# A transformer block on one core: row sums in column tiles of 32, three unused products at the passage to attention, and one subtraction moved to GpSimd

## The chip, the cores and the metric

The kernel runs on one core of one Trainium2 chip. The metric is the device time of one execution in microseconds (us). Engines are named as in the profile: PE is TensorE's matrix multiplication, PEld its weight load, DVE is VectorE, ACT is ScalarE, POOL is GpSimd, SP is SyncE, which issues nearly all DMAs.

## What is computed

A block of 2048 tokens by 576 features, in float32. Six vectors of modulation come from one row `c`; attention has 32 heads of 18 with one shared key and value; the mixer part is a two-layer MLP with a hidden size of 4608.

```python
mod = (silu(c) @ w_mod).reshape(1, 6, 1, 576)
sa, ca, ga, sb, cb, gb = (mod[:, i] for i in range(6))
h = layernorm(x) * (1 + ca) + sa
q, k, v = h @ wq, h @ wk, h @ wv                  # 32 heads of q, one of k and v
p = softmax(q @ k.T * 18 ** -0.5)
x = x + ga * ((p @ v) @ wo)
h = layernorm(x) * (1 + cb) + sb
x = x + gb * (gelu(layernorm(h) @ w1 + b1) @ w2 + b2)
```

## The kernel before, in words

The program is one long recording with the order of every engine written out by hand. It has three stages, each with its own division of the eight PSUM banks.

**Stage 1** (up to about 129 us) normalizes x, multiplies by the projection weights in four blocks of 512 tokens (`q_chunk`), and begins the row maxima that the softmax needs. A `unit()` is one such piece for the second quad of heads: four products (L319) into two double banks `psA`, and a `tensor_reduce` on DVE for each (L337). The last unit stands at the very end of the stage. `busy(n)` (L391) multiplies the identity by itself n times into a bank `psB` that nobody reads; the kernel uses it three times near the start.

**Stage 2** (129 us to about 1387 us) is attention, in 32 quads of four heads. A list of tokens (`QUAD`, later `QUADW`) sets the order: S is a product of scores (L901, into one of four banks `psB`, read by an exponential on ACT, L903), M a product for the maxima of the next quad (L319, into one of three banks `psM`, read by a reduction on DVE, L923), X a corrected maximum (L911, L914, L921), V a number of 128-column pieces of the product of probabilities and values. V has 32 stationary columns, so four of them stand side by side in column tiles of PE (L891). F1 and F2 finish the maxima of the next quad; F2 is one small transposing product (L357), so its record marks a fixed place in every quad. After every second block of keys a step of a list of side work (`fill`) is taken, just behind the V product. In the first quads the side work is `late_weights`: four of the modulation rows are made here, not in stage 1. POOL scales a 576 x 576 matrix by silu(c) and adds its five slices (L498, L501); what is left is a sum over 128 partitions, whose result every partition needs. `bcast` (L516 to L523) makes it: a product with a stationary 128 x 128 matrix of ones, 288 columns at a time into two banks (L521), and a `tensor_scalar` on DVE for each half (L522). Rows 5, 2 and 3 are made in the quad n = 1, row 4 in n = 2. Row 2 (`gab`) then scales the output weights (L550).

**Stage 3** (from 1387 us) is the MLP, for two halves of the tokens, with Strassen-like sums of blocks: `op_pieces` forms the operands from the normalized rows. `form("=T4")` is a subtraction of two 128 x 1024 blocks (L1016), `-B21` and the like are the low parts of operands (L1025). For the first half of the tokens `e2` is DVE for all sums; for the second half, formed in step v = 17, `e2` is POOL, and of the three subtractions only `=T1` runs on `e2`.

SP takes its DMAs in the order in which they are written; a DMA that waits keeps all later ones waiting. On SP stand in stage 2 the loads of queries (L315), the rows of maxima (L364), the modulation matrices (L527, L92) and the output weights (L540).

Of the kernel before, what the change touches and what calls it, by code (L numbers as in the profile page):

```python
# [32 lines left out]
def block_kernel(ctx: ExitStack, tc, x, wqkv, wo, w1, b1, w2, b2, c, wmod, ident_in, out):  # L33
    nc = tc.nc
    ve, ac, po, pe, sy = nc.vector, nc.scalar, nc.gpsimd, nc.tensor, nc.sync

    per = ctx.enter_context(tc.tile_pool(name="per", bufs=1))
    dr = ctx.enter_context(tc.tile_pool(name="dr", bufs=1, space=bass.MemoryType.DRAM))
# [14 lines left out]
    def psB(): return PS["t"].tile([128, 512], F32, name="psB", bufs=PS["b"])  # L53
# [3 lines left out]
    def big(): return per.tile([128, 10, 512], F32R, name="big", bufs=3)  # L57
# [17 lines left out]
    BC = per.tile([128, 3, D], F32, name="BC")  # L75
# [36 lines left out]
    unity = pa.tile([128, 128], F32, name="unity")  # L112
# [157 lines left out]
    def q_chunk(tb, m, zt, mid, n):  # L270

        w = 126 if m < KD - 1 else 128
        wd = 126 if m < KD - 1 else 72
        pq = psB()
        proj(pq[:w], wqh, wql, 126 * m, 126 * m + w, zt, mid, n)
        qs = p1.tile([128, 2, TB], F32R, name="qs", bufs=2)
        qf = p1.tile([128, TB], F32, name="qf", bufs=2)
        ac.activation(qf[:w], pq[:w], AF.Copy)
        ac.activation(qs[:w, 0], pq[:w], AF.Copy)
        po.tensor_tensor(qs[:w, 1], qf[:w], qs[:w, 0].bitcast(F32), op=ALU.subtract)  # L280
        if m == KD - 1:
# [47 lines left out]
    def smax_half(n, u, half):  # L329
        p, qt = UNITS[u]  # L330
        ts = psA(), psA()
        for i in range(2):
            for g in range(2):
                smax_mm(n, ts[g][:, i, :], g, p, qt, 2 * half + i)
        for g in range(2):
            k, ax = (slice(2 * half, 2 * half + 2), AX.X) if g == 0 or half == 0 else (slice(2, 3), AX.XY)
            ve.tensor_reduce(mx_tile(n)[:, 8 * g + 4 * p + qt, k], ts[g], axis=ax, op=ALU.max)  # L337
# [52 lines left out]
    def busy(n):  # L390

        p = psB()
        for _ in range(n):
            pe.matmul(p[:, :128], ident, ident, start=True, stop=True)
# [42 lines left out]
    def unit():  # L437
        nonlocal u1
        smax_half(1, u1 % 2, u1 // 2)
        u1 += 1  # L440
# [5 lines left out]
    for tb in range(NB):  # L446
        nz = big() if tb + 1 < NB else None
        for i, m in enumerate((4, 0, 1, 2, 3)):
            np_ = NPART[tb][i]
            if i == 2:  # L450
                parts.extend((u, tb) for u in range(8))
            mid = {(NB - 1, 1): unit, (NB - 1, 4): lambda: last.popleft()()}.get((tb, i), part)
            qf, qs = q_chunk(tb, m, zt, mid, np_ + 1 if np_ else 0)
            if i == 0:
                qv = qf, qs
            if i == 1:
                k_block(tb, qv[1])
                v_block(tb, qv[0])
                if tb == 0:
                    load_q(0)  # L460
            if i == 2:
                if tb == 0:
                    load_q(1)
            if tb == NB - 1:
                if i == 0:
                    unit()
                elif i == 3:
                    smax_fin1(0)
                if i == 4:
                    unit()  # L470
            if nz is not None:
                for k in {1: (0, 1, 2), 2: (3, 4)}.get(i, ()) if tb else {3: (0, 1, 2), 4: (3, 4)}.get(i, ()):
                    h_chunk(tb + 1, nz, k)
            if tb < 2:
                for _ in range(NSTAT[tb][i]):
                    ln1_stats(*stats.popleft())
                for _ in range(NAPPLY[tb][i]):
                    b, t = applies.popleft()
                    ln1_apply(b, t, ve if b == 1 else ac)
        zt = nz  # L480
# [5 lines left out]
    px = pxp.__enter__()  # L486
# [2 lines left out]


    WO, YR, ATT, B2 = {}, {}, {}, {}

    def late_weights():

        gab = pb.tile([128, D], F32, name="gab", tag="r2", bufs=3)

        def scaled(w, k0, k1):
            po.tensor_tensor(w[:, k0:k1], w[:, k0:k1], st[:, k0:k1, None].to_broadcast([128, k1 - k0, D]), op=ALU.mult)  # L498

        def added(w, k0, k1, n=1):  # L500
            po.tensor_tensor(w[:, k0:k0 + n], w[:, k0:k0 + n], w[:, k1:k1 + n], op=ALU.add)  # L501

        def total(w):

            scaled(w, 0, 2)
            yield
            scaled(w, 2, 4)
            yield
            scaled(w, 4, 5)
            added(w, 0, 2, 2)  # L510
            yield
            added(w, 0, 1)
            added(w, 0, 4)
            yield

        def bcast(w, dst, add, scl):  # L516

            for h2 in range(2):
                cs = slice(288 * h2, 288 * (h2 + 1))
                p = psB()  # L520
                pe.matmul(p[:, :288], unity, w[:, 0, cs], start=True, stop=True)  # L521
                ve.tensor_scalar(dst[:, cs], p[:, :288], scl, add, op0=ALU.mult, op1=ALU.add)  # L522
            yield  # L523

        m3, m2, m5 = (bigw(D) for _ in range(3))
        for j, t in ((5, m5), (2, m2), (3, m3)):
            sy.dma_start(t, wmod[j])  # L527
        yield
        sums = (x for t in (m5, m2, m3) for x in total(t))
        rows = (x for a in ((m5, BC[:, 2, :], 0.0, 0.5), (m2, gab, 0.0, 1.0), (m3, BC[:, 0, :], 0.0, 1.0))  # L530
                for x in bcast(*a))
        for i in range(12):
            for _ in range(2):
                next(sums, None)
            if i > 5 and i % 2:
                next(rows)
            yield
        m4 = load_mod(4)
        wor = bigw(D)
        sy.dma_start(wor, wo)  # L540
        ATT[0] = big()
        yield
        yield from total(m4)
        yield
        yield
        yield from bcast(m4, BC[:, 1, :], 1.0, 1.0)
        wos = pw.tile([128, 2, KD, D], F32R, name="wos", tag="wA", padded_shape=[128, 2, KD, WQC])
        WOH, WOL = WO["h"], WO["l"] = wos[:, 0], wos[:, 1]
        for k in range(KD):
            po.tensor_mul(wor[:, k, :], wor[:, k, :], gab)  # L550
            po.tensor_copy(WOH[:, k, :], wor[:, k, :])
            po.tensor_tensor(WOL[:, k, :], wor[:, k, :], WOH[:, k, :].bitcast(F32), op=ALU.subtract)
            yield
# [396 lines left out]
    for n in range(NQT):  # L950
# [54 lines left out]
    def op_pieces(R, e2):  # L1005


        at = {"B11": (0, 0, ve), "B21": (2, 2, e2), "B22": (4, 7, e2), "T2": (6, 5, ve), "T1": (8, 5, ve),
              "T3": (10, 0, ve), "T4": (12, 2, e2), "t0": (0, 4, ve), "t1": (1, 9, ve)}
        less = {"T3": (5, 0, 0), "T4": (2, 5, 2), "T1": (7, 5, 5)}  # L1010

        def form(what):
            for w in what.split():
                if w[0] == "=":
                    x, y, o = (R[:, i:i + 2] for i in less[w[1:]])
                    (e2 if w == "=T1" else ve).tensor_tensor(o, x, y, op=ALU.subtract)  # L1016
                    continue
                a, r, e = at[w[1:]]
                n = 2 if w[1] in "BT" else 1
                o, lo = (OP, 14) if n == 2 else (TL[0], 2)  # L1020
                hi, src = o[:, a:a + n], R[:, r:r + n]
                if w[0] == "+":
                    ac.activation(hi, src, AF.Copy)
                else:
                    e.tensor_tensor(o[:, lo + a:lo + a + n], src, hi.bitcast(F32), op=ALU.subtract)  # L1025
        return form
# [31 lines left out]
    px = ctx.enter_context(tc.tile_pool(name="mx", bufs=1, side="right", reuse_waits="tile"))  # L1058
# [256 lines left out]
    for v in range(NV):  # L1315
# [44 lines left out]
        bc = psB()  # L1360
# [111 lines left out]
```

## Time and profile before

| what | value |
|---|---|
| median of 3 runs | 2242.26 us (2241.82 to 2245.19) |
| profiled execution | 2243.08 us |
| its span, first to last instruction | 2241.3 us |
| outside the span | 1.8 us |
| busy PE, DVE, ACT, POOL | 2212.7, 1940.8, 1645.1, 1524.7 us |
| mean granted clock of TensorE | 0.998 |

A row of the timeline has the start, the time covered, engine, line, operation, tiles, shape and count; in brackets the idle time of the engine ahead of it and what ended that. A row of a window has the stretch, its length, the busy time of PE, PEld, DVE, ACT and POOL with their instruction counts, then the granted clock, the share of DMA time and GB/s. PE works on a float32 product in two passes, so one product of such operands has two records.

### The profile page before, as it was taken

The page shows a single profiled execution, that of the slowest core. Times are in us where ns is not written, and L with a number is a line of the kernel's source. Part 1 is how long each engine was busy: PE and PEld are TensorE (multiplying, and loading weights), DVE is VectorE, ACT ScalarE, POOL GpSimd, SP SyncE. Part 2 cuts the span into 40 slices and gives each one's busy share as a digit, 9 for nine tenths or more (in the row PEclk, how much of TensorE's full clock was granted, in tenths as well). Part 3 has the DMA queues.
Part 4 walks back from the last instruction along what each step waited for, and adds up shares of the span by engine and source line. Part 5 has one row for each costly group of instructions (what it writes and reads, how often), then busy time and mean ns, then how long its engine had stood idle before and what let it go on. Part 6 is the DMA issues. An engine that isn't in the chain of part 4 may idle for free.

```text
span 2241.3 us, 45781 instructions
## 1 busy us (share of the span) xinstructions
PE 2212.7 (99%) x16458; PEld 1442.2 (64%) x16458; DVE 1940.8 (87%) x3420; ACT 1645.1 (73%) x3145; POOL 1524.7 (68%) x1760
## 2 busy tenths in 40 slices
PE   7999999999999999999999999999999999999999
PEld 5644544444444544444444445888888888989898
DVE  7589999999999999999999982887888878888787
ACT  5569999999999999999999997444545544344443
POOL 6654356776877787777776300888888857877776
PEclk9999999999999999999999999999999999999999
DMA  6232034443433333343333101666666646676664
GB/s 229 85 129 75 15 114 138 133 142 110 138 121 126 121 122 115 124 139 115 117 127 127 49 13 48 194 177 179 180 178 176 190 122 181 182 213 191 177 183 125
DMA packets 182404, 303.79 MB, mean 136 GB/s; under 512 B 19243, under 2 KB 74923, under 8 KB 182177
## 3 DMA queue, kind: packets, MB, share of 16 engines
q1 hardware_dynamic: 182033, 300.72, 42.9%
q8 instruction: 130, 2.13, 0.4%
q14 instruction: 97, 0.79, 0.1%
q10 hardware_dynamic: 144, 0.15, 0.0%
HBM read 198.71 MB, written 93.19 MB: 130 GB/s over the span
## 4 chain that ended last, share of the span: by engine, by line
PE 86%; DVE 3%; ACT 3%; POOL 2%; issue 1%; DMA 0%; SPq 0%; POOLq 0%; ACTq 0%
PE psC L891 21%; PE psB L1111 18%; PE psA L1214 16%; PE psB L901 13%; PE psM L319 10%; PE psB L700 2%; ACT P L903 2%; PE psB L911 2%; DVE mx L923 1%; PE psA L1248 1%; PE psA L700 1%; DVE xc L921 0%; PE psB L155 0%; PE psB L357 0%; PE psB L248 0%
## 5 line engine op out<-in xcount | busy, mean ns | idle before, releaser
L903 ACT ACTIVATE P<-psB 128x512 f32<-128x512 f32 x2008 | 1043.8, 619 | 35.0 <-PE psM L319 12.3
L923 DVE TENSOR_REDUCE mx<-psM 128x1 f32<-128x512 f32 x1476 | 938.1, 683 | 37.5 <-PE psM L319 14.9
L319 PE MATMUL psM<-KS,qst 64*128 64x512 f32 x1722 | 601.2, 442 | 0.4 <-DVE mx L923 0.4
L901 PE MATMUL psB<-qst,KS 64*128 64x512 f32 x2008 | 585.1, 429 | 1.7 <-DVE mx L337 1.5
L891 PE MATMUL psC<-P,V 128*32 128x256 f32 (+3 forms) x6424 | 576.3, 448 | 0.5 <-ACT O L715 0.5
L901 PEld LDWEIGHTS psB<-qst,KS 64*128 64x128 f32 x2008 | 303.4, 185 | 218.2 <-ACT P L903 141.3
L1111 PE MATMUL psB<-ops,w1a 128*128 128x512 f32 x1512 | 393.8, 396 | 0.2 <-DVE h L1126 0.2
L319 PEld LDWEIGHTS psM<-KS,qst 64*128 64x128 f32 x1722 | 275.6, 184 | 161.9 <-DVE mx L923 120.4
L1111 PEld LDWEIGHTS psB<-ops,w1a 128*128 128x128 f32 x1512 | 270.1, 188 | 46.6 <-DVE h L1126 0.6
L891 PEld LDWEIGHTS psC<-P,V 128*32 128x32 f32 x6424 | 140.0, 108 | 200.1 <-issue 173.4
L1220 DVE TENSOR_TENSOR XT<-psA,XT 128x576 f32<-128x576 f32 x330 | 241.7, 753 | 19.0 <-PE psA L1214 13.6
L1214 PEld LDWEIGHTS psA<-w2s,big 128*128 128x128 f32 x1584 | 223.0, 188 | 13.9 <-POOL big L1188 2.5
L1214 PE MATMUL psA<-w2s,big 128*128 128x288 f32 x1584 | 230.4, 294 | 0.0
L1124 ACT ACTIVATE psB<-gs 128x512 f32<-128x512 f32 x144 | 86.7, 602 | 130.0 <-DVE gs L1123 130.0
L1188 POOL TENSOR_TENSOR big<-s,big 128x512 fp32r<-128x512 f32 x132 | 170.9, 1295 | 10.6
L1120 ACT ACTIVATE h<-psB,b1t 128x512 f32<-128x512 f32 x144 | 97.9, 680 | 102.5 <-PE psB L1111 81.8
L921 DVE CUSTOM_DVE_ANT_0 xc<-psM,xc 128x512 f32<-128x512 f32 x246 | 165.8, 680 | 3.6 <-PE psB L901 1.5
L914 ACT ACTIVATE xc<-psB 128x512 f32<-128x512 f32 x246 | 152.8, 621 | 8.8 <-PE psM L319 7.4
L735 POOL TENSOR_TENSOR os<-O,os 128x512 fp32r<-128x512 f32 x28 | 36.1, 1289 | 164.8 <-ACT os L734 164.8
L1123 DVE SCALAR_TENSOR_TENSOR gs<-psB,h 128x512 f32<-128x512 f32 x144 | 98.5, 684 | 39.5 <-ACT psB L1121 39.4
L762 POOL TENSOR_TENSOR r<-r,r 128x256 fp32r<-128x256 f32 (+1 forms) x162 | 121.6, 751 | 13.0
L1129 ACT ACTIVATE big<-h 128x512 fp32r<-128x512 f32 x39 | 24.7, 633 | 133.7 <-DVE h L1126 133.7
(214 smaller groups left out, 3341.2 us busy)
## 6 DMA issues: line engine op xcount, KB each, us to landing
w1a<-w1scr SPq DMA_DIRECT2D x252, 256.0 KB
w2s<-w2sum SPq DMA_DIRECT2D x132, 288.0 KB
w1scr<-r SPq DMA_DIRECT2D x126, 256.0 KB
w2s<-w2scr SPq DMA_DIRECT2D x76, 288.0 KB
w2scr<-r SPq DMA_DIRECT2D x72, 288.0 KB
w2sum<-r SPq DMA_DIRECT2D x72, 288.0 KB
qst<-qscr SPq DMA_DIRECT2D x192, 72.0 KB
w1a<-w2scr SPq DMA_DIRECT2D x33, 288.0 KB
```

What stands on the lines that cost most here:

```text
L319: pe.matmul(o, QST[n][64 * g:64 * g + 64, p, 128 * qt:128 * (qt + 1)], KS[64 * g:64 * g + 64, 512 * kb:512 * (kb + 1)], start=True, stop=True)
L762: po.tensor_tensor(o[:, n:2 * n], src, o[:, :n].bitcast(F32), op=ALU.subtract)
L891: pe.matmul(PVt[n][32 * j:32 * (j + 1), cs], V[:, kc, :], t[:, j, cs], start=(kc == 0 and h0 == 0), stop=(kc == 15), skip_group_check=True)
L901: pe.matmul(t, KS[64 * g:64 * g + 64, 128 * kc:128 * (kc + 1)], QST[n][64 * g:64 * g + 64, i, :], start=True, stop=True)
L903: ac.activation(P[n, kc][:, 2 * i + g, :], t, AF.Exp, scale=SCALE)
L914: ac.activation(XC[-1], t, AF.Relu)
L921: ve.tensor_tensor_reduce(c, t, c, 1.0, -3.0e38, ALU.add, ALU.max, o)
L923: ve.tensor_reduce(o, t, axis=AX.X, op=ALU.max)
L1111: pe.matmul(o, x, y, start=(first and i == 0), stop=(i == len(terms) - 1), skip_group_check=True)
L1188: po.tensor_tensor(unit(u, 1), x, unit(u, 0).bitcast(F32), op=ALU.subtract)
L1214: pe.matmul(p[:, i, :288], x[:, ts_], W2S[k][:, y], start=(bool(first) and q == 0), stop=(q == 2), skip_group_check=True)
L1220: ve.tensor_tensor(o, p[:, :, :288], o, op=ALU.add)
```

## The change

Three edits, told in the order of the program.

1. The passage: the last unit of stage 1 has one unused product ahead of it and two behind it.
2. The rows: `bcast` now makes its sum with 32 stationary columns of ones. Four products of 144 columns stand in four column tiles of one bank, so that partitions 32j to 32j+31 hold the piece j of the row; one `tensor_scalar` of 144 columns reads the bank; a DMA writes one partition of each piece to memory, and in the next step of the side work a second DMA reads the row back into all 128 partitions. A row now takes two steps instead of one, begins a step earlier, and the third of each pair of DMAs stands on SP ahead of the loads of row 4's matrix and of the output weights.
3. `=T4` runs on `e2`. With the first half's `form` that is DVE as before, so one instruction moves, in v = 17.

```diff
                 if i == 4:
+                    busy(1)
                     unit()
+                    busy(2)
...
-        def bcast(w, dst, add, scl):
-
-            for h2 in range(2):
-                cs = slice(288 * h2, 288 * (h2 + 1))
-                p = psB()
-                pe.matmul(p[:, :288], unity, w[:, 0, cs], start=True, stop=True)
-                ve.tensor_scalar(dst[:, cs], p[:, :288], scl, add, op0=ALU.mult, op1=ALU.add)
+        def bcast(n, w, dst, add, scl):
+
+            p = psB()
+            for j in range(4):
+                pe.matmul(p[32 * j:32 * (j + 1), :144], unity[:, :32], w[:, 0, 144 * j:144 * (j + 1)], start=True, stop=True,
+                          skip_group_check=True)
+            r = px.tile([128, 144], F32, name="bc", tag="r" + "3543"[n], padded_shape=[128, (256, 256, D, 256)[n]])
+            ve.tensor_scalar(r, p[:, :144], scl, add, op0=ALU.mult, op1=ALU.add)
+            sy.dma_start(rowscr[n].rearrange("o (j c) -> (o j) c", j=4), r.rearrange("(j p) c -> j p c", p=32)[:, 0, :])
+            yield
+            sy.dma_start(dst, rowscr[n].to_broadcast([128, D]))
             yield
...
-            if i > 5 and i % 2:
+            if i > 5:
                 next(rows)
...
-                    (e2 if w == "=T1" else ve).tensor_tensor(o, x, y, op=ALU.subtract)
+                    (ve if w == "=T3" else e2).tensor_tensor(o, x, y, op=ALU.subtract)
```

Lines of the changed kernel are 2 higher from the passage on and 8 higher behind `bcast`: L901 becomes L909, L891 L899, L1016 L1024, L1132 L1140.

PE at the passage, before. L319 is the last unit of maxima, L901 the first score of attention:

```order
L248 MATMUL psB<-big,wA 126x512 x4
L319 MATMUL psA<-KS,qst 128x512 x4
L901 MATMUL psB<-qst,KS 128x512
L319 MATMUL psM<-KS,qst 128x512
L901 MATMUL psB<-qst,KS 128x512 x2
```

The same place in the change:

```order
L248 MATMUL psB<-big,wA 126x512 x4
L394 MATMUL psB<-ident 128x128
L319 MATMUL psA<-KS,qst 128x512 x4
L394 MATMUL psB<-ident 128x128 x2
L909 MATMUL psB<-qst,KS 128x512
L319 MATMUL psM<-KS,qst 128x512
```

The three products with the identity (L394) are new; nothing else is in another place.

PE in the quad n = 1, around the first row, before. L891 is V, L521 the sum:

```order
L901 MATMUL psB<-qst,KS 128x512
L891 MATMUL psC<-P,V 32x256 x4
L521 MATMUL psB<-bigw,unity 128x288 x2
L319 MATMUL psM<-KS,qst 128x512
L901 MATMUL psB<-qst,KS 128x512 x2
```

The first row in the change, a step of the side work earlier, and the third, which falls between two pieces of V:

```order
L899 MATMUL psC<-P,V 32x256 x4
L524 MATMUL psB<-bigw,unity 32x144 x4
L909 MATMUL psB<-qst,KS 128x512 x2
L319 MATMUL psM<-KS,qst 128x512
...
L899 MATMUL psC<-P,V 32x128 x4
L524 MATMUL psB<-bigw,unity 32x144 x4
L899 MATMUL psC<-P,V 32x256 x4
```

All four sums stand directly behind a V, which has 32 stationary columns too.

SP behind the loads of the first quads, in the change (the six rows with `rowscr` are new, the others were there in this order):

```order
L364 DMA qst<-ms 1x8x128 x4
L528 DMA rowscr_1280<-bc 4x144
L315 DMA qst<-qscr 18x2x512 x6
L530 DMA BC<-rowscr_1280 128x576
L528 DMA rowscr_1281<-bc 4x144
L530 DMA gab<-rowscr_1281 128x576
L528 DMA rowscr_1282<-bc 4x144
L530 DMA BC<-rowscr_1282 128x576
L92 DMA bigw<-in_wmod 128x5x576
L548 DMA bigw<-in_wo 128x5x576
L364 DMA qst<-ms 1x8x128 x4
```

The loads L92 and L548 (L540 before) now come behind the third read of a row.

POOL in v = 17, in the change. L1033 is `-B21`, L1140 the low part of a GELU's result; before, there was one L1016 in this place, behind the second L1132:

```order
L1033 TENSOR_TENSOR ops<-yr,ops 128x1024
L1140 TENSOR_TENSOR big<-h,big 128x512
L1024 TENSOR_TENSOR yr<-yr 128x1024
L1140 TENSOR_TENSOR big<-h,big 128x512
L1024 TENSOR_TENSOR yr<-yr 128x1024
```

The first L1024 is `=T4`, the second `=T1`, which was on POOL already.

More of the change, by code (lines that the diff above doesn't have):

```diff
@@ L491, in block_kernel @@
     WO, YR, ATT, B2 = {}, {}, {}, {}
+    rowscr = [dr.tile([1, D], F32, name="rowscr%d" % n) for n in range(4)]
     def late_weights():
@@ L529, in late_weights @@
         sums = (x for t in (m5, m2, m3) for x in total(t))
-        rows = (x for a in ((m5, BC[:, 2, :], 0.0, 0.5), (m2, gab, 0.0, 1.0), (m3, BC[:, 0, :], 0.0, 1.0))
+        rows = (x for a in ((0, m5, BC[:, 2, :], 0.0, 0.5), (1, m2, gab, 0.0, 1.0), (2, m3, BC[:, 0, :], 0.0, 1.0))
                 for x in bcast(*a))
@@ L545, in late_weights @@
         yield
-        yield from bcast(m4, BC[:, 1, :], 1.0, 1.0)
+        yield from bcast(3, m4, BC[:, 1, :], 1.0, 1.0)
         wos = pw.tile([128, 2, KD, D], F32R, name="wos", tag="wA", padded_shape=[128, 2, KD, WQC])
```

## The prediction

> **What bounds the kernel now.** I read the page first, for the engine that sets the time.
>
> ```profile
> span 2241.3 us, 45781 instructions
> PE 2212.7 (99%) x16458; PEld 1442.2 (64%) x16458; DVE 1940.8 (87%) x3420; ACT 1645.1 (73%) x3145; POOL 1524.7 (68%) x1760
> PE 86%; DVE 3%; ACT 3%; POOL 2%; issue 1%; DMA 0%; SPq 0%; POOLq 0%; ACTq 0%
> ```
>
> PE is busy nearly all the time and holds 86% of the chain that ended last. So an edit is worth what it takes from PE's line of work, either time of its own or a hole. I looked up the three places of the change: windows and timeline at the passage, the fixed mark of each quad for the rows, and the timeline of v = 17.
>
> First the passage, in windows of 3.41 us (busy times of PE, PEld, DVE, ACT, POOL, then the granted clock):
>
> ```profile
> 128.05:131.46 3.41, 1.92 (x10) 0.99 (x9) 3.15 (x4) 1.22 (x3) 0.57 (x1) 1.00 0.52 146
> 131.46:134.87 3.41, 3.06 (x13) 1.96 (x12) 3.41 (x7) 3.40 (x7) 0.00 (x0) 0.50 0.76 197
> 134.87:138.28 3.41, 3.41 (x17) 1.03 (x14) 1.27 (x3) 1.90 (x5) 0.00 (x0) 0.50 1.03 382
> 138.28:141.70 3.42, 3.42 (x29) 1.22 (x26) 3.26 (x6) 3.05 (x7) 2.49 (x2) 1.00 1.06 391
> ```
>
> Attention begins at half clock: 0.50 from 131.46 to 138.28. The window ahead of it has PE busy for 1.92 of 3.41 us. PE's rows there, two later V products among them:
>
> ```profile
> 126.22 0.50 PE L319 MATMUL psA<-KS,qst 64*128 64x512 f32 x1 [0.19 <-DVE mx L337]
> 127.35 0.73 PE L319 MATMUL psA<-KS,qst 64*128 64x512 f32 x3 [0.63 <-DVE mx L337]
> 129.17 0.50 PE L901 MATMUL psB<-qst,KS 64*128 64x512 f32 x1 [1.09 <-DVE mx L337]
> ...
> 135.39 1.93 PE L891 MATMUL psC<-P,V 128*32 128x512 f32 x8
> 138.60 1.06 PE L891 MATMUL psC<-P,V 128*32 128x512 f32 x8
> ```
>
> The holes are waits for DVE, which still reduces the last unit. Then the first V takes 1.93 us, the second 1.06.
>
> **The passage.** The three new products cost nothing if they fit the holes. A product of 128 columns with the identity as moving side is the mark of each quad, and the V behind it starts 0.21 us later (161.23 to 161.44):
>
> ```profile
> 161.23 0.28 PE L357 MATMUL psB<-ident,mxf 128*16 128x128 f32 x1
> 161.44 1.07 PE L891 MATMUL psC<-P,V 128*32 128x256 f32 x16
> 202.43 0.28 PE L357 MATMUL psB<-ident,mxf 128*16 128x128 f32 x1
> 241.12 0.28 PE L357 MATMUL psB<-ident,mxf 128*16 128x128 f32 x1
> 278.54 0.28 PE L357 MATMUL psB<-ident,mxf 128*16 128x128 f32 x1
> ```
>
> One product (0.21) stands ahead of the unit's first, which idles 0.19 anyway; two (0.42) stand behind the unit, in the hole of 1.09 us that ends when DVE is done. Without that cover they would cost 0.6 us. They write banks `psB`, for which nothing waits at this place. What they may bring is activity: with 0.42 us more, the window before the fall has 2.34 of 3.41 us, 69% instead of 56%.
>
> If the clock stays up, PE gets the following back. From the first V's start to the second's are 3.21 us (135.39 to 138.60); the same pieces, V, X, three M and two S, take 1.90 in the next quad, from 175.30 to 177.20:
>
> ```profile
> 175.30 1.06 PE L891 MATMUL psC<-P,V 128*32 128x512 f32 x8
> 177.20 1.06 PE L891 MATMUL psC<-P,V 128*32 128x512 f32 x8
> ```
>
> That is 1.31 us. Ahead of it DVE and ACT are busy for 3.41 and 3.40 of 3.41 us, so a faster PE gains little there. From above I bound the gain by what ACT idles in this stretch, since ACT's own work before it can't be moved:
>
> ```profile
> 138.08 0.60 ACT L914 ACTIVATE xc<-psB 128x512 f32<-128x512 f32 x1 [1.51 <-PE psM L319]
> 140.13 1.09 ACT L903 ACTIVATE P<-psB 128x512 f32<-128x512 f32 x2 [0.28 <-PE psM L319]
> ```
>
> 1.51 + 0.28 = 1.79 us. So the term lies between 0 (the clock falls all the same) and 1.8; I take 1.5, between the two estimates.
>
> A rule speaks against it. The Trainium skill ("TensorE: Matmul & The Clock Gate", Part 1: The HAM clock gate) says that the clock is either half or full, that it is judged in free-running windows of about 3.4 us, and that it returns to half after an idle window. The two levels and the length (131.46 to 138.28 is two such windows) agree with the trace; the idle window doesn't, since PE was busy 56% of the window before the fall. By the page's rule 0.6 us of products would change nothing, and where its windows fall against the program would differ from run to run. So the fall depends on a level of activity that no row gives; a fall that stays is a rival below.
>
> **The rows.** What a row costs on the path is read from the marks. From 161.23 to 202.43 are 41.20 us with three rows, from 202.43 to 241.12 38.69 with one, from 241.12 to 278.54 37.42 with none. One row is 1.27 us, three are 3.78 (1.26 each), together 5.05 us for four. On PE:
>
> ```profile
> 165.45 0.64 PE L891 MATMUL psC<-P,V 128*32 128x256 f32 x8
> 166.02 0.50 PE L319 MATMUL psM<-KS,qst 64*128 64x512 f32 x1
> 173.09 1.24 PE L521 MATMUL psB<-bigw,unity 128*128 128x288 f32 x4
> 183.81 1.24 PE L521 MATMUL psB<-bigw,unity 128*128 128x288 f32 x4
> 184.97 0.42 PE L891 MATMUL psC<-P,V 128*32 128x128 f32 x8
> 185.33 0.50 PE L319 MATMUL psM<-KS,qst 64*128 64x512 f32 x1
> ```
>
> L521 holds PE for 1.16 us (183.81 to 184.97). The new sum has the form of V: eight records, four side by side in two rounds. A V of 256 columns holds PE for 0.57 us (165.45 to 166.02), one of 128 for 0.36 (184.97 to 185.33): 0.21 per 128 columns and 0.15 for entering and leaving. As all four new sums stand behind a V, 0.15 isn't paid again: 144/128 x 0.21 = 0.24 us. On PE alone a row thus falls from 1.26 to 0.24.
>
> Whether ACT and DVE let that through:
>
> ```profile
> 173.88 0.94 DVE L522 TENSOR_SCALAR BC<-psB 128x288 f32<-128x288 f32 x2
> 174.82 1.08 ACT L903 ACTIVATE P<-psB 128x512 f32<-128x512 f32 x2 [0.81 <-PE psB L901]
> 185.90 0.60 ACT L914 ACTIVATE xc<-psB 128x512 f32<-128x512 f32 x1 [1.18 <-PE psM L319]
> 196.58 3.65 ACT L903 ACTIVATE P<-psB 128x512 f32<-128x512 f32 x7 [1.27 <-PE psM L319]
> ```
>
> ACT idles about 1.1 us behind each row, so it follows. DVE's 0.94 us become one `tensor_scalar` of half the columns, under 0.46 us. The new row costs at least 0 and, if DVE's 0.46 is what counts, at most 0.46: the saving is 3.2 to 5.05 us. I take 4.0, near PE's own 4 x (1.26 - 0.24) = 4.1.
>
> The six new DMAs of the first three rows, and two for the fourth, stand on SP. What comes late is the load of row 4's matrix:
>
> ```profile
> 174.69 0.60 SPq L92 DMA_DIRECT2D bigw<-in_wmod  x1
> 139.21 5.28 POOL L498 TENSOR_TENSOR bigw<-bigw,st 128x1152 f32<-128x1152 f32 x3 [10.59 <-DMA bigw<-in_wmod]
> 205.74 4.17 POOL L498 TENSOR_TENSOR bigw<-bigw,st 128x1152 f32<-128x1152 f32 x2
> 243.21 1.29 POOL L735 TENSOR_TENSOR os<-O,os 128x512 fp32r<-128x512 f32 x1 [19.50 <-ACT os L734]
> ```
>
> The rows begin a step, half of 183.81 - 173.09, earlier: about 167.7, 178.5 and 189.5. With two to three us from the third sum to its landed write, L92 comes near 192 instead of 174.69. The first three matrices, issued from about 131.7, let POOL start at 139.21, 7.5 us later; so row 4's is there near 200, and POOL takes it at 205.74, or near 201 after the gains. The cover is thin, but behind it POOL idles 19.5 us; a late start there costs nothing. I price the DMAs at 0.
>
> **=T4.** In v = 17:
>
> ```profile
> 1804.66 2.31 DVE L1016 TENSOR_TENSOR yr<-yr 128x1024 f32<-128x1024 f32 x1 [0.81 <-POOL ops L1025]
> 1805.81 0.62 PE L1111 MATMUL psB<-opt,w1a 128*128 128x512 f32 x2
> 1807.69 0.66 PE L1248 MATMUL psA<-w2s,big 128*128 128x288 f32 x3 [1.26 <-DVE XT L1285]
> 1804.59 1.29 POOL L1132 TENSOR_TENSOR big<-h,big 128x512 fp32r<-128x512 f32 x1
> 1811.00 1.68 POOL L1132 TENSOR_TENSOR big<-h,big 128x512 fp32r<-128x512 f32 x1 [5.12 <-ACT big L1129]
> ```
>
> DVE waits 0.81 us for POOL, subtracts for 2.31, and only then releases the bank that PE wants: a hole of 1.26 us on PE. The subtraction's own length and its wait, 3.12 us, are more than the hole, so without it DVE releases the bank in time. On POOL it runs from 1805.8, behind L1132, and the one `=T1` that POOL has lasts 2.42 us: it ends near 1808.3, inside an idle time of 5.12 us. With PE 1.3 us earlier there, 1.5 us of that cover remain; gone, a late GELU part would cost PE the excess. Saving 0.8 to 1.4, I take 1.3.
>
> **Sum** against the profiled execution of 2243.08 us (span 2241.3 and 1.8 around it; the median is 0.82 lower): 4.0 + 1.3 + 1.5 = 6.8, so 2236.3. The other runs may have lost less at the passage, so part of the 0.82 counts: I predict **2236.0 us**. What is saved early reaches the end because PE is nearly without holes behind it.
>
> **Rivals.**
>
> - *The clock falls all the same.* For it: the rule above, and a window that may lie differently; against it: the activity rises to 69%. Time 2243.08 - 5.3 = 2237.8.
> - *The rows' gain stays with ACT and DVE.* A bank of `psB` is held until DVE comes to the sum, behind up to three reductions; were a row still to cost 0.94 us as DVE's two did, the saving were 4 x 0.32 = 1.3 and the time, without the clock's gain, 2240.5. Against it stands ACT's idle time behind each row.
> - *SP becomes the bound, and the kernel slower.* A read of a row waits on SP until its write has landed, and behind the third pair wait L92, L548 and the rows of maxima (L364), without which the scores of the next quad can't start. Near 192 the pair should be through, and L364 was issued at 203.94 (near 199 after the gains): some 5 us are left once L92 and L548 are issued. Each us beyond delays PE by one. It decides when the pairs hold SP 12 us longer than reckoned, 5 of slack and 6.8 of gain; at 17 us more the time would be 2247.5. Nothing in the trace shows such a landing for 2 KB.
> - *No effect*: the three places are shorter, and what follows waits for something that doesn't move. Time 2242. Against it: the quads with fewer rows are shorter.
>
> **How the numbers follow.** Forecast 0.55, clock falls 0.24, gain with ACT and DVE 0.12, SP 0.03, no effect 0.06. About 0.2% (4.5 us) is what a measurement of this kernel can tell from no change; from 2242.26 that is 2237.8. The forecast's terms give 2243.08 - 3.2 - 0.8 - 0 = 2239.1 at worst and 2243.08 - 5.05 - 1.4 - 1.8 = 2234.8 at best; 0.8 lower for the median, and as much again for its own spread, is 2233.2. At the upper end the range goes on to the third case, 2240.5. It then leaves out the last two cases and little else. Faster: the forecast, and half of the second case, which lies on the bound, 0.67. Same: the other half, the third and the fifth, 0.30. Slower: 0.03.
>
> **What would show it.** The granted clock at 1.00 between 128 and 142 us, and 1.9 us between the first two V; the marks of the first quads 38.1 and 37.7 us apart where they were 41.2 and 38.7, with ACT's idle times behind the rows gone; no hole on PE near 1800 us, and on POOL two L1024. Wrong: half clock at the passage again, new waits of POOL or PE for a DMA of a modulation matrix or of maxima, or quads that are still over 39 us long.

## The result, and the profile after

The changed kernel takes **2237.2 us** (median of 12 runs, 2235.38 to 2237.78) beside 2242.09 us for the kernel before on the same chip (12 runs, 2240.18 to 2245.31): a ratio of 0.9977 with a 95% interval of 0.9969 to 0.9985, or 4.9 us less. Forecast were 2236.0 us, range 2233.2 to 2240.5. The profiled execution took 2237.57 us, 5.51 less than the one before.

The page of the changed kernel, as it was shown for the kernel before:

```profile
span 2235.7 us, 45834 instructions
PE 2209.9 (99%) x16480; PEld 1440.9 (64%) x16480; DVE 1935.7 (87%) x3415; ACT 1645.4 (74%) x3145; POOL 1528.7 (68%) x1761
PE 88%; DVE 3%; ACT 3%; issue 1%; POOL 0%; ACTq 0%; POOLq 0%; DVEq 0%
```

PE still bounds it, and POOL's 2% have left the chain. The rest has to be looked up at the three places.

**The rows.** PE's mark of each quad, after:

```profile
122.02 0.27 PE L357 MATMUL psB<-ident,mxf 128*16 128x128 f32 x1
160.88 0.28 PE L357 MATMUL psB<-ident,mxf 128*16 128x128 f32 x1
199.34 0.28 PE L357 MATMUL psB<-ident,mxf 128*16 128x128 f32 x1
237.19 0.28 PE L357 MATMUL psB<-ident,mxf 128*16 128x128 f32 x1
274.54 0.28 PE L357 MATMUL psB<-ident,mxf 128*16 128x128 f32 x1
```

From mark to mark are 38.86, 38.46, 37.85 and 37.35 us, where they were 38.42, 41.20, 38.69 and 37.42 (the mark ahead of those shown was at 122.81). The quad with three rows is 2.74 shorter, that with one 0.84. A row still costs (38.46 - 37.35)/3 = 0.37 us in the first and 0.50 in the second. PE and DVE at the third row, which falls between two V:

```profile
188.61 0.43 PE L524 MATMUL psB<-bigw,unity 128*32 128x144 f32 x8
188.86 0.61 PE L899 MATMUL psC<-P,V 128*32 128x256 f32 x8
```
```profile
189.66 0.30 DVE L527 TENSOR_SCALAR bc<-psB 128x144 f32<-128x144 f32 x1
```

On PE the sum holds 0.25 us here (188.61 to 188.86), as worked out (0.24); DVE's operation takes 0.30 us, and comes 1.05 us after the sum has begun. ACT's idle time behind the first row is now 0.38 us, where 0.81 to 1.27 were shown:

```profile
168.92 1.57 ACT L911 ACTIVATE P<-psB 128x512 f32<-128x512 f32 x3 [0.38 <-PE psB L909]
```

**SP.** The third row's two DMAs, and the load of row 4's matrix behind them, L92 (L528 writes a row, L530 reads it back):

```profile
189.98 0.51 SPq L528 DMA_DIRECT2D rowscr<-bc  x1
191.57 0.31 SPq L530 DMA_DIRECT2D BC<-rowscr  x1
191.94 0.63 SPq L92 DMA_DIRECT2D bigw<-in_wmod  x1
```
```profile
201.41 1.28 POOL L743 TENSOR_TENSOR os<-O,os 128x512 fp32r<-128x512 f32 x1 [22.08 <-ACT os L742]
202.64 4.17 POOL L502 TENSOR_TENSOR bigw<-bigw,st 128x1152 f32<-128x1152 f32 x2
```

A read follows its write by 1.6 us. L92 goes out at 191.94 (forecast: near 192), and POOL takes row 4's matrix (L502) directly behind its work before, with no wait of its own: the cover was there.

**=T4.** POOL and PE in v = 17:

```profile
1800.49 1.29 POOL L1140 TENSOR_TENSOR big<-h,big 128x512 fp32r<-128x512 f32 x1
1801.74 2.41 POOL L1024 TENSOR_TENSOR yr<-yr 128x1024 f32<-128x1024 f32 x1
1804.40 1.28 POOL L1140 TENSOR_TENSOR big<-h,big 128x512 fp32r<-128x512 f32 x1 [0.25 <-ACT big L1137]
```
```profile
1801.70 0.63 PE L1119 MATMUL psB<-opt,w1a 128*128 128x512 f32 x2
1802.17 0.57 PE L1256 MATMUL psA<-w2s,big 128*128 128x288 f32 x3
```

The subtraction stands inside POOL's idle time, of which 0.25 us are left, and PE goes from L1119 to L1256 without the hole of 1.26 us.

**The passage.** Windows (busy PE, PEld, DVE, ACT, POOL, granted clock) and PE's rows:

```profile
124.87:128.28 3.41, 2.45 (x12) 1.37 (x10) 2.81 (x4) 1.08 (x2) 1.27 (x1) 1.00 0.37 121
128.28:131.69 3.41, 2.43 (x13) 1.20 (x13) 3.15 (x6) 2.23 (x5) 0.00 (x0) 1.00 0.68 201
131.69:135.10 3.41, 3.41 (x14) 1.86 (x18) 3.41 (x6) 3.41 (x7) 0.00 (x0) 0.50 0.89 258
135.10:138.51 3.41, 3.41 (x18) 1.03 (x14) 1.27 (x3) 1.59 (x4) 0.17 (x1) 0.50 1.05 393
```
```profile
126.57 0.73 PE L319 MATMUL psA<-KS,qst 64*128 64x512 f32 x3 [0.63 <-DVE mx L337]
127.24 0.71 PE L394 MATMUL psB<-ident 128*128 128x128 f32 x4
128.40 0.49 PE L909 MATMUL psB<-qst,KS 64*128 64x512 f32 x1 [0.45 <-DVE mx L337]
...
134.61 1.93 PE L899 MATMUL psC<-P,V 128*32 128x512 f32 x8
138.05 1.26 PE L899 MATMUL psC<-P,V 128*32 128x512 f32 x8
```

The clock falls again for 6.83 us, from 131.69 to 138.51. The two products (L394) fit their hole, but stand in the window before the one that led to the fall; that one, 128.28 to 131.69, holds only the first scores and maxima, and PE is busy for 2.43 us of it, more than the 2.34 that the prediction hoped to reach with the products. The first two V are 3.44 us apart, not 1.9, and the first quad is 0.44 us longer than before.

**Where the 5.6 us of the span are.** Ahead of the first mark 0.8 (122.81 against 122.02), which no edit touches and which is chance: the first mark of the runs below lies between 121.3 and 125.1. The passage adds 0.44, the rows take off 2.74 and 0.84. From the last mark (1342.35 before, 1338.72 after) to the end the time falls from 898.95 to 896.98, 2.0 us. Stage 2 behind the rows' quads gives back 0.3; why is not shown.

### The profile page after: what moved, and what is told of

It reads as the page before. It is cut to its first block, busy times and chain, and to the rows that moved or that the text cites. A ratio compares the mean times of both kernels' runs of the same rounds, so it can differ in the third digit from the quotient of the medians.

```text
span 2235.7 us, 45834 instructions
## 1 busy us (share of the span) xinstructions
PE 2209.9 (99%) x16480; PEld 1440.9 (64%) x16480; DVE 1935.7 (87%) x3415; ACT 1645.4 (74%) x3145; POOL 1528.7 (68%) x1761
## 4 chain that ended last, share of the span: by engine, by line
PE 88%; DVE 3%; ACT 3%; issue 1%; POOL 0%; ACTq 0%; POOLq 0%; DVEq 0%
PE psC L899 22%; PE psB L1119 18%; PE psA L1222 16%; PE psB L909 14%; PE psM L319 10%; PE psB L708 2%; ACT P L911 2%; PE psB L919 2%; PE psA L1256 1%; DVE mx L931 1%; PE psA L708 1%; DVE xc L929 1%; PE psB L155 0%; PE psB L357 0%; PE psB L248 0%
## 5 line engine op out<-in xcount | busy, mean ns | idle before, releaser
L319 PE MATMUL psM<-KS,qst 64*128 64x512 f32 x1722 | 601.3, 442 | 0.5 <-DVE mx L931 0.4
L909 PE MATMUL psB<-qst,KS 64*128 64x512 f32 x2008 | 585.4, 429 | 1.2 <-DVE mx L337 0.9
L899 PE MATMUL psC<-P,V 128*32 128x256 f32 (+3 forms) x6424 | 576.5, 448 | 0.5 <-ACT O L723 0.5
L909 PEld LDWEIGHTS psB<-qst,KS 64*128 64x128 f32 x2008 | 303.6, 185 | 217.2 <-ACT P L911 140.6
L1119 PE MATMUL psB<-ops,w1a 128*128 128x512 f32 x1512 | 393.8, 396 | 0.2 <-DVE h L1134 0.2
L319 PEld LDWEIGHTS psM<-KS,qst 64*128 64x128 f32 x1722 | 275.6, 184 | 162.6 <-DVE mx L931 121.9
L1119 PEld LDWEIGHTS psB<-ops,w1a 128*128 128x128 f32 x1512 | 270.1, 188 | 46.7 <-DVE h L1134 0.6
L899 PEld LDWEIGHTS psC<-P,V 128*32 128x32 f32 x6424 | 140.2, 108 | 200.7 <-issue 173.5
L1132 ACT ACTIVATE psB<-gs 128x512 f32<-128x512 f32 x144 | 86.7, 602 | 127.8 <-DVE gs L1131 127.7
```

What stands on the lines that cost most here:

```text
L319: pe.matmul(o, QST[n][64 * g:64 * g + 64, p, 128 * qt:128 * (qt + 1)], KS[64 * g:64 * g + 64, 512 * kb:512 * (kb + 1)], start=True, stop=True)
L899: pe.matmul(PVt[n][32 * j:32 * (j + 1), cs], V[:, kc, :], t[:, j, cs], start=(kc == 0 and h0 == 0), stop=(kc == 15), skip_group_check=True)
L909: pe.matmul(t, KS[64 * g:64 * g + 64, 128 * kc:128 * (kc + 1)], QST[n][64 * g:64 * g + 64, i, :], start=True, stop=True)
L1119: pe.matmul(o, x, y, start=(first and i == 0), stop=(i == len(terms) - 1), skip_group_check=True)
```

## The experiments

Eleven kernels ran, each beside the kernel before on its chip (medians of that between 2241.95 and 2242.34 us). Unused products and operations come on top of the kernel's work, and what they write is read by nobody. My theory at the start: PE's line of work prices the rows and =T4, and the clock falls when a window of 3.41 us has too little activity. The rivals: DVE or the held bank prices the rows; the clock falls whatever is put there.

### The three edits one by one

Only the rows (the second edit of the change):

> Only the row sums changed; passage and =T4 as before. Theory (the rows carry most of the gain): the first two full quads last 38.4 and 37.8 us from mark to mark, as in the changed kernel (before: 41.2 and 38.7), so 3.6 us less than before, 2238.5 us; the hole of 1.3 us on PE in step v = 17 is still there. Rival (the rows' gain needs the other edits, or part of it is the passage): less than 2.5 us, or quads over 39 us.

Measured: 2240.03 us, ratio 0.9989 (0.998 to 0.9998). The marks are 38.43, 38.43, 37.84 and 37.40 us apart, so 2.76 + 0.86 = 3.6 us, as in the changed kernel. The median shows only 2.1; the interval, 0.4 to 4.5 us, holds both.

Only the passage:

```diff
                 if i == 4:
+                    busy(1)
                     unit()
+                    busy(2)
```

> Only the three unused products at the passage. Theory (they don't raise the activity enough in the window that counts, so the clock falls to half all the same for 6.8 us): within 0.5 us of before, and half clock in the profile between about 131 and 138 us. Rival (they hold the clock up in most executions, and the profiled one was an exception): 1.5 us less than before, 2240.6, with most clocks at 0.999, and the first two V products 1.9 us apart.

Measured: 2241.28 us, ratio 0.9995 (0.9986 to 1.0004). In its profile the clock was at half from 130.41 to 137.24, although the two products stood at 128.20, inside the window of 127.0 to 130.41 that came before. So the fall isn't only a matter of the products lying a window too early.

Only =T4:

```diff
-                    (e2 if w == "=T1" else ve).tensor_tensor(o, x, y, op=ALU.subtract)
+                    (ve if w == "=T3" else e2).tensor_tensor(o, x, y, op=ALU.subtract)
```

> Only =T4 moved to GpSimd. Theory (it takes the wait of PE for a bank away and brings no new one): the hole on PE in v = 17 is gone, 1.3 us less than before, 2240.8 us. Rival (a later GELU part on GpSimd gives it back): a new wait of PE or ACT for GpSimd within the next 30 us, and the time of before within 0.5 us.

Measured: 2240.54 us, ratio 0.9995 (0.9986 to 1.0004), so 1.6 us by the medians, inside the uncertainty. The trace says more: the hole is gone, and from the last mark to the end are 896.9 us. Over all of these profiles that stretch is 898.6 to 899.0 without the edit (before, rows only, passage only) and 896.9 to 897.0 with it (=T4 only, changed kernel, and the one that follows).

The changed kernel without the three products:

> The changed kernel without the three unused products. Theory (they do nothing): the changed kernel's time within 0.7 us, 2236.5 to 2237.9, with half clock for 6.8 us at the passage. Rival (they save some of the half clock in part of the executions): 0.7 to 1.5 us more than the changed kernel, 2238 to 2238.7.

Measured: 2237.28 us, ratio 0.9978 (0.9969 to 0.9987): the same as with them. **What the three products bring is too little for the medians to show**; the counts further down put it near 0.3 us. Its windows:

```profile
125.88:129.29 3.41, 1.92 (x9) 1.00 (x10) 2.92 (x3) 0.60 (x1) 1.21 (x1) 1.00 0.37 104
129.29:132.70 3.41, 3.41 (x13) 1.73 (x12) 3.07 (x7) 3.38 (x7) 0.00 (x0) 0.50 0.72 199
```

The fall comes behind a window with 1.92 us of PE, as in the kernel before.

### More products at the passage

Nine, three of them inside the last unit, on top of the changed kernel:

```diff
+    gap = [False]
...
                 smax_mm(n, ts[g][:, i, :], g, p, qt, 2 * half + i)
+                if gap[0] and i == 0 and g == 0:
+                    busy(3)
...
                 if i == 4:
                     busy(1)
+                    gap[0] = True
                     unit()
-                    busy(2)
+                    gap[0] = False
+                    busy(5)
```

> The changed kernel with the holes ahead of attention filled: one unused product ahead of the last unit, three inside it and five behind it, nine instead of three. Theory (a level of activity decides, and the three products were too few): the clock stays at 1.00 through the passage and the time is 1.5 us under the changed kernel's, about 2235.5. Rival 1 (the stretch of scores and maxima that follows has too little activity by itself): the clock falls at 131 to 135 us all the same and the time is that of the changed kernel, 2237.2. Rival 2 (the products delay the unit or attention): first score over 0.5 us later against the last projection, and a time over 2237.7.

Measured: 2236.56 us, ratio 0.9976 (0.9966 to 0.9985). In its profile the clock fell for one window only, and the window ahead of that was the one with the first scores and maxima:

```profile
126.61:130.02 3.41, 3.16 (x21) 2.15 (x20) 2.95 (x3) 0.71 (x2) 0.91 (x1) 1.00 0.44 122
130.02:133.43 3.41, 2.76 (x16) 1.11 (x13) 3.25 (x6) 3.41 (x8) 0.00 (x0) 1.00 0.72 199
133.43:136.84 3.41, 3.41 (x15) 1.05 (x15) 1.62 (x3) 1.98 (x5) 0.00 (x0) 0.50 1.04 370
```

With the last unit's window at 3.16 us of PE, the clock fell behind the next one (2.76 us), where PE waits for DVE's maxima. So filling the hole at the last unit is not enough.

The same, and eight more among the first nine maxima of attention:

```diff
+        nm = 0
         for tok in order:
+            if n == 0 and tok[0] == "M":
+                nm += 1
...
                 if unit:
                     mx_mm(*unit, tok[0], int(tok[1]))
+                if n == 0 and tok[0] == "M" and nm in (1, 4, 5, 6, 7, 8, 9):
+                    p = psC()
+                    for _ in range(2 if nm == 1 else 1):
+                        pe.matmul(p[:, :128], ident, ident, start=True, stop=True)
```

> As the fourth experiment, and with eight more unused products among the first nine maxima of attention, the stretch in which the clock fell there (133.4 to 136.8). Theory (a level of activity in each window decides): the clock stays at 1.00 from 25 us to the end, the first two V products stand 1.9 us apart, the mark of the quad n = 0 comes 1.5 us sooner after the mark before it than in the changed kernel (37.3 instead of 38.9 us), and the time is 2235.5 to 2236. Rival (something other than activity brings the fall, for instance the change from products of 128 rows to products of 64): half clock again between 130 and 138 us and no gain over the fourth experiment's 2236.6.

Measured: 2239.36 us, ratio 0.9988 (0.9979 to 0.9997). In its profile the clock is at 1.00 from 25.43 us to the end, but the time is longer. PE's rows (L915 scores, L319 maxima, L1002 the added products, L905 V):

```profile
134.54 0.50 PE L915 MATMUL psB<-qst,KS 64*128 64x512 f32 x1
134.88 0.39 PE L319 MATMUL psM<-KS,qst 64*128 64x512 f32 x1
135.20 0.49 PE L1002 MATMUL psC<-ident 128*128 128x128 f32 x2
135.62 0.50 PE L915 MATMUL psB<-qst,KS 64*128 64x512 f32 x1
...
138.19 1.06 PE L905 MATMUL psC<-P,V 128*32 128x512 f32 x8
```

A score, a maximum and an added product take 1.08 us (134.54 to 135.62); a score and a maximum alone came every 0.60 us in the passage of other kernels, where DVE, which reads the maxima, is busy for 3.25 to 3.41 us of a window. Here the score (64 rows) no longer runs beside the maximum: they start 0.34 us apart. The product itself holds 0.42 us. From first score to first V are 8.42 us, where the version with nine has 5.99. So with every window filled the clock stayed up in this profile, and eight products buy that for more than it is worth.

Three single products instead of the eight (behind the maxima 4, 6 and 8):

> The changed kernel with nine unused products around and inside the last unit of maxima, and three more single ones among the maxima of the first quad (behind the fourth, sixth and eighth), where the version with eight kept the clock at 1.00 and lost 2.8 us to the products. If the clock falls by a level of activity in a window of 3.41 us (my theory), three products raise PE's busy time there by about 1.3 us of the 6 to 8 us between first score and first V: the window may stay up in some executions, and the products cost 3 x 0.45 = 1.3 us where each costs what it did before; so the time is between 2236.6 (the version with nine) and 2239.4 (with eight more), near 2237.5, and no better than the changed kernel. If the loss of the version with eight was mostly another thing (the two products in the first place, or the longer chain), three cost nothing and the clock's 1.7 us come as a gain: 2235.

Measured: 2236.32 us, ratio 0.9975 (0.9965 to 0.9986), the lowest median here, yet no difference to the changed kernel (0.9977) that the intervals allow. In its profile the clock stayed at 1.00, and the first quad took 37.25 us against 38.86 in the changed kernel.

How often the clock stayed up can be estimated from the mean granted clock of all executions. A mean of 0.999 or more leaves at most 6.7 us at half in the whole execution. Two windows at the passage alone are 6.83, and eleven of the thirteen profiles spend one or two more near the program's start. The measure errs both ways: a profile below with 0.999 lost one window at the passage (320 columns on DVE), another with 0.998 none (the bank read twice more). A mean of 0.999 was reached in 0 of 96 executions of the kernel before, in 0 of 32 of the three changed kernels without products, in 14 of 67 of the six with three products, in 9 of 17 of those with nine to twelve, in 7 of 11 with seventeen. In the changed kernel it was 4 of 12, with a median of 2235.75 us; the other eight have 2237.35. So the three products do something: 14 of 67 against none of 128 without them. At 1.6 us each time that is some 0.3 us on the average, an estimate from these counts.

### What a row costs

An unused product of 288 columns and 128 stationary columns behind each sum, in the same bank:

```diff
+            pe.matmul(p[:, 144:432], unity, w[:, 0, :288], start=True, stop=True, skip_group_check=True)
             r = px.tile([128, 144], F32, name="bc", tag="r" + "3543"[n], padded_shape=[128, (256, 256, D, 256)[n]])
```

> The changed kernel with one more unused product at each row, of the kind of before (128 stationary columns, 288 moving), so that PE's time for a row rises by 0.48 us of products and a change of the stationary width, about 0.6 us, and DVE's stays. Theory (PE is what a row costs): the first two full quads last about 40.2 and 38.5 us, and the time rises by 2.4 us to 2239.6. Rival (there is slack on PE behind a row): quads under 39 us, and the changed kernel's time.

Measured: 2240.09 us, ratio 0.9988 (0.9979 to 0.9997). The quads take 40.32 and 38.31 us: 0.62 more a row, and 0.46 for the fourth. The third row:

```profile
190.38 0.43 PE L524 MATMUL psB<-bigw,unity 128*32 128x144 f32 x8
190.74 0.75 PE L526 MATMUL psB<-bigw,unity 128*128 128x288 f32 x2
191.42 0.64 PE L900 MATMUL psC<-P,V 128*32 128x256 f32 x8
```

It holds PE for 0.68 us (190.74 to 191.42), of which 0.62 count in the first of the two quads and 0.46 in the second.

Two unused `tensor_scalar`s of 320 columns on DVE, reading a tile in SBUF:

```diff
             ve.tensor_scalar(r, p[:, :144], scl, add, op0=ALU.mult, op1=ALU.add)
+            waste = pb.tile([128, 320], F32, name="waste", bufs=1)
+            for _ in range(2):
+                ve.tensor_scalar(waste, KS[:, :320].bitcast(F32), scl, add, op0=ALU.mult, op1=ALU.add)
```

> The changed kernel with two more tensor_scalars of 128x320 on DVE at each row, so that a row takes DVE about as long as before (0.8 to 0.9 us) and PE as in the change. Theory (PE is what a row costs): the first two full quads last at most 38.9 and 38.0 us from mark to mark. Rival (DVE's work counts as much): the 0.5 us come on top at each row, 40 and 38.4 us, and the time rises by 2 us to 2239.

Measured: 2239.98 us, ratio 0.999 (0.9982 to 0.9999), quads of 41.60 and 38.02 us. That is 3.15 us over the changed kernel for three rows and only 0.17 for one, which fits neither theory. I first put it down to the operations being longer than planned, at all rows; the last run shows that only the first row's were.

Two of 144 columns, reading the row's own bank:

```diff
+            waste = pb.tile([128, 144], F32, name="waste", bufs=1)
+            for _ in range(2):
+                ve.tensor_scalar(waste, p[:, :144], scl, add, op0=ALU.mult, op1=ALU.add)
```

> The changed kernel with two more tensor_scalars of 128x144 from the row's own bank (into a tile that nobody reads) behind each row's own one. In the changed kernel that operation took 0.30 us, so DVE gets about 0.6 us more a row, and the bank of psB is released that much later; PE gets nothing. If PE sets what a row costs (my theory), the first marks stay 38.5 and 37.8 us apart, within 0.3, and the time stays within 1 us of the changed kernel. If DVE sets it (the rival), each row costs 0.6 more: 40.2 and 38.4, and 2.4 us over the changed kernel. The run with two wasted operations of 2.7 us together a row added 1.05 us a row and can't tell this, since it was longer than any slack.

Measured: 2238.07 us, ratio 0.9979 (0.997 to 0.9988). The medians can't tell it from the changed kernel, but the marks can. The quads take 39.74 and 38.37 us, +1.28 for three rows and +0.52 for one, where PE alone would have left them as they were. PE's marks, PE's wait behind the third row, and DVE's rows there:

```profile
158.09 0.28 PE L357 MATMUL psB<-ident,mxf 128*16 128x128 f32 x1
197.83 0.28 PE L357 MATMUL psB<-ident,mxf 128*16 128x128 f32 x1
236.20 0.28 PE L357 MATMUL psB<-ident,mxf 128*16 128x128 f32 x1
...
188.66 0.47 PE L912 MATMUL psB<-qst,KS 64*128 64x512 f32 x1 [0.26 <-DVE waste L530]
```
```profile
187.66 0.30 DVE L527 TENSOR_SCALAR bc<-psB 128x144 f32<-128x144 f32 x1
187.87 0.64 DVE L530 TENSOR_SCALAR waste<-psB 128x144 f32<-128x144 f32 x2
188.43 1.28 DVE L934 TENSOR_REDUCE mx<-psM 128x1 f32<-128x512 f32 x2
```

Of 0.56 us more on DVE (187.87 to 188.43), 0.43 and 0.52 come through. The way is seen too: a score waits 0.26 us for the bank that the added operations hold. At the other three rows a score waits 0.45, 0.18 and 0.22 us, by the trace for ACT to free a bank; in the changed kernel the trace has no such wait in these quads. **My theory of PE alone falls.** This kernel has the changed kernel's passage, untouched, and in its profiled execution the clock did not fall:

```profile
126.81:130.22 3.41, 2.50 (x13) 1.37 (x13) 3.15 (x4) 1.32 (x3) 0.46 (x1) 1.00 0.54 151
130.22:133.63 3.41, 2.83 (x16) 1.30 (x20) 3.41 (x7) 3.41 (x8) 0.00 (x0) 1.00 0.78 218
```
```profile
133.56 1.07 PE L902 MATMUL psC<-P,V 128*32 128x512 f32 x8
135.45 1.06 PE L902 MATMUL psC<-P,V 128*32 128x512 f32 x8
```

The first two V are 1.89 us apart, and the first quad takes 36.62 us: 1.8 less than the kernel before with its 38.42. So a clock that stays up is worth what I had reckoned; this is one profile, and the counts above say how seldom it came.

The same two operations, but from the tile that the row's operation has written, so that the bank is free at once:

```diff
+            waste = pb.tile([128, 144], F32, name="waste", bufs=1)
+            for _ in range(2):
+                ve.tensor_scalar(waste, r, scl, add, op0=ALU.mult, op1=ALU.add)
```

> The changed kernel with two more tensor_scalars of 128x144 behind each row's own one, as in the run before last, but from the tile that the row's operation has written, not from its bank: DVE gets about 0.5 us more a row, and the bank of psB comes free when the row's own operation is done. There each row cost 0.43 to 0.52 us more by the marks, which my theory of PE alone did not expect. If what costs is the bank that is held longer (the rival of the prediction in its words), the marks go back to 38.5 and 37.8, within 0.15. If it is DVE's time itself, whatever it reads, they stay near 39.7 and 38.4. The run with 2.7 us a row on DVE, which held no bank, added 1.05 and 0.17: that speaks for a part of both, 38.8 and 38.0 here.

Measured: 2239.72 us, ratio 0.9987 (0.9978 to 0.9996), quads of 41.52 and 37.98 us. The fourth row pays 0.13 of 0.47 us (0.17 with 320 columns, which held no bank either): most of what it paid in the run before came from the held bank. The three rows pay 3.07 us, which neither theory had, and the reason stands at the first of them:

```profile
170.76 0.30 DVE L527 TENSOR_SCALAR bc<-psB 128x144 f32<-128x144 f32 x1
171.09 2.72 DVE L530 TENSOR_SCALAR waste<-bc 128x144 f32<-128x144 f32 x2
173.73 1.27 DVE L934 TENSOR_REDUCE mx<-psM 128x1 f32<-128x512 f32 x2
```
```profile
168.08 5.64 POOL L505 TENSOR_TENSOR bigw<-bigw 128x1152 f32<-128x1152 f32 x3
```
```profile
174.46 1.10 PE L319 MATMUL psM<-KS,qst 64*128 64x512 f32 x2 [1.41 <-DVE mx L934]
```

These two take 2.64 us (171.09 to 173.73) while POOL adds its slices (L505, to 173.72), and 0.23 us each at the other rows, where POOL has no such operation. The two of 320 columns took 1.29 and 1.46 us at the same place, beside 0.33 at the others. DVE's maxima come late behind them, and PE waits 1.41 us for one. From the first row's DVE operation to the second's are 11.08 us (8.80 in the changed kernel, 11.02 with 320 columns, 9.16 from the bank); from the second to the third 12.31 (11.98, 12.38, 12.41). So the first row gives 2.3 of the 3.07 us, by DVE's stand beside POOL, and each later row of this quad pays 0.33 to 0.46 of its 0.47 us even with the bank free, though the trace prints no wait of PE there.

## Why the prediction was right, and where not

- **What bounds the kernel.** Right: what was taken from PE's line of work, by the rows and by =T4, came through to the end but for 0.3 us.
- **The rows** were priced at 4.0 us (3.2 to 5.05) and gave 3.6 by the marks. PE's part was right: the sum holds PE for 0.25 us where another V follows. At the other three, where a score follows, it holds PE for 0.36 (168.03 to 168.39 at the first), and the V ahead of the first one is 0.11 shorter for it (0.46 instead of 0.57). The mis-sized step is "near PE's own 4 x (1.26 - 0.24)". A row costs about the longer of its two operations, PE's sum and DVE's read of the bank, and 0.1 on top: 1.26 for 1.16 and 0.94 us before, 0.37 to 0.50 for 0.25 to 0.36 and 0.30 after, 0.96 to 0.99 with an added 0.68 on PE, 0.80 to 1.02 with an added 0.56 on DVE. With PE's sum this short, DVE's bound (0.46 in the prediction) was the nearer one. That fit is mine, from five cases, and argued rather than shown. The run with the bank free lies off it: by its 0.77 us on DVE the fourth row should cost 0.87, and it costs 0.63. How much of DVE's part is the bank and how much DVE's own time differs between the two quads (0.13 of 0.47 us in one, 0.3 or more in the other with the bank free).
- **The rows' DMAs** were priced at 0, and cost nothing. L92 was put near 192 us and came at 191.94; POOL didn't wait for it. The rival with SP as the bound had no part.
- **=T4** was priced at 1.3 us (0.8 to 1.4) and gave about 1.6: matched product by product, PE's lead over the kernel without it grows by 1.6 us at this place (from 0.47 to 2.08 us against the kernel before, over 5319 products behind the last mark). The mechanism held; the hole that the trace prints, 1.26 us, was too small a measure. It counts from the end of L1111, which reaches into the next product. From start to start L1111 to L1248 take 1.88 us before (1805.81 to 1807.69) and 0.47 after (1801.70 to 1802.17), so 1.41 are saved there and the last 0.19 within the next 4 us.
- **The passage** was priced at 1.5 us and gave nothing in the profile, some 0.3 on the average. The step that failed is "with 0.42 us more, the window before the fall has 2.34 of 3.41 us": the windows stand elsewhere against the program in each execution, the products were in an earlier window in the profiled one, and where they were inside (passage alone, 2.10 of 3.41 us, and the run with the bank free, 2.43) the clock fell too. The rival "the clock falls all the same", with 2237.8 us, describes what most executions did; a clock that stays up is worth 1.6 to 1.8 us, so the size of the gain was right and the chance given to it too high.
- **The sum.** 3.6 + 1.6 + 0 = 5.2 us against 6.8, and 0.3 are given back behind the rows. The time fell 4.9 by the medians. That it lies in the range does not confirm the forecast: the range held the rival without the clock's gain too, and 2237.2 us are nearer to its 2237.8 than to 2236.0.

The clock gate as the Trainium skill has it ("TensorE: Matmul & The Clock Gate", Part 1: The HAM clock gate) was half right here. Its free-running windows of about 3.4 us hold: every half-clock stretch at the passage is 3.41 or 6.83 us long, at another place of the program in each execution. Its idle window as the condition for the fall does not: at the passage no window ahead of a fall had less than 1.92 us of PE, and near 45 us the clock stayed up behind a window with 1.69 (passage alone, from 45.08). (In two profiles it also fell once elsewhere, near 48 us, behind windows with 0.87 and 1.43.)

## What to carry to other kernels

Work that is added to hold a clock must fill every window that may be the weak one, since the windows don't stand still against the program. It pays only where it costs less than the clock brings, so first price it among the products that it stands between. When an engine's operation gets much shorter, price what remains by the next engine in the same chain, here DVE, which reads the bank and holds it. And measure a kernel's parts by marks that are fixed in the program: medians could not tell edits of 1 to 2 us apart, distances of marks could.

## What was not expected of the hardware

- At the passage the clock fell behind windows in which PE was busy from 1.92 to 2.77 of 3.41 us, and stayed up behind others with 2.50 and 2.83, and near 45 us with 1.69. PE's busy time alone does not order them; what the gate counts stays open. Products of 128 rows among those of 64 don't settle it either: the window with 2.50 us holds two of the three added ones and the clock stayed, the one with 2.43 in the run with the bank free holds the same two and it fell.
- In the run with eight more, a product of 128 rows between a maximum and the next score, both of 64 rows, held PE for 0.42 us, and the pair, which otherwise starts together, was parted: with the product it took 1.08 us where the pair alone came every 0.60.
- A `tensor_scalar` on DVE from SBUF to SBUF took 1.2 to 1.5 us instead of 0.23 (144 columns) or 0.33 (320) while POOL ran a `tensor_tensor` of 128 x 1152 in SBUF, until that ended. From PSUM the same operation took 0.30 us beside the same kind of operation of POOL (166.31 in the run with the bank, POOL busy with L505 from 165.04 to 167.69). The Trainium skill ("SBUF — State Buffer", SBUF: two separate sides) tells of a pair of ports that some of DVE's operations and GpSimd's lock against each other for a whole instruction; the traces agree.
